# Attention sum of a sliding, dilated attention moved to (offset, head) on partitions, with the values re-laid through DRAM

## The chip, the cores and the metric

The kernel runs on one core of a Trainium2 chip. The metric is the device time of one execution in microseconds (us). The profiler's span of the same execution, first to last instruction, is 1 to 2 us shorter than that time, and positions inside the kernel are given on the span. A ratio is always the mean time of one kernel's fast runs over that of the other's fast runs of the same rounds on the same chip, so it is not quite the ratio of the medians that I quote.

TensorE does matrix multiplies, VectorE elementwise work, ScalarE evicts accumulators and does exponentials, GpSimd a few masks, and DMA queues move data. In the profile they are PE (with PEld for its weight loads), DVE, ACT, POOL and, for the queue that issues transfers, SP.

## The reference, cut to what matters

```python
# x: [2048, 640]; 32 heads of 20; window of 8 offsets with step 2
xn = layernorm(x)
q, k, v = split(xn @ wqkv)                     # each [32 heads, 2048, 20]
idx = pos[:, None] - 2 * arange(8)[None, :]    # position minus 0, 2, ... 14
logits = einsum("bhsd,bhswd->bhsw", q, k[idx]) * 20 ** -0.5     # masked where idx < 0
attn = softmax(logits, axis=-1)                # over the 8 offsets
o = einsum("bhsw,bhswd->bhsd", attn, v[idx])
h = (xn @ w_gate) * (xn @ w_up)                # gated part, inner size 1536
return x + o @ wo + h @ w_down
```

Softmax runs over 8 offsets only. The attention sum `o` is therefore no matrix product: it is, for each of 640 channels and 2048 positions, a sum of eight products.

## The kernel before

It keeps everything transposed: channel on partitions (five chunks of 128), position along the row. Attention weights are computed with (position block, head) on partitions, one row per offset `w`, in `LOG`. To multiply them with the values, they have to be repeated over the 20 channels of each head. That is done by TensorE with a 0/1 matrix `GTZ`, one matmul for each offset, chunk and block of 512 positions. Then ScalarE evicts, VectorE multiplies by the shifted values, and TensorE adds the eight products with an identity matrix:

```python
    units = [(w, c, j) for j in range(NJ) for c in range(NCH) for w in range(W)]     # 4 x 5 x 8 = 160

    def pv_E(u):
        ...
        op("pe", lambda e: e.matmul(PS[:, eb, :], GTZ[:, j, c, :], LOG[:, w, :], start=True, stop=True), ...)
        op("act", lambda e: e.activation(ES[:, es, :], PS[:, eb, :], ACT.Copy), ...)
        lo = PAD + j * JB - DIL * w
        op("dve", lambda e: e.tensor_tensor(PB[:, pb, :], ES[:, es, :], VTP[:, c, lo:lo + JB], ALU.mult), ...)

    def pv_I(u):
        ...
        op("pe", lambda e: e.matmul(PS[:, ob, :], IDENT[:], PB[:, pb, :], start=(w == 0), stop=(w == W - 1)), ...)
        if w == W - 1:
            op("act", lambda e: e.activation(QOT[:, c, j * JB:(j + 1) * JB], PS[:, ob, :], ACT.Copy), ...)
```

The order of work is: layer normalization together with the Q, K and V projections; the logit stage (40 VectorE products of 128x2048, each followed by four 32-column logit matmuls), with gate and up matmuls between; softmax; the attention stage above, with the rest of the gated part and the output projection between.

## Time and profile before

| | before |
|---|---|
| time, median of 4 runs | 352.55 us (351.58 to 353.38) |
| span of the profiled run | 351.9 us |
| TensorE busy | 334.8 us, 95% |
| VectorE, ScalarE busy | 60%, 58% |
| mean granted TensorE clock | 1.000 |

The profile's page of the kernel before: its busy line, the chain of work that ended last, and four of the costliest groups (line, engine, operation, output and inputs, count | busy us, mean ns of one | idle us just before them and who ended it).

```profile
PE 334.8 (95%) x1884; PEld 158.9 (45%) x1884; DVE 212.7 (60%) x438; ACT 203.2 (58%) x362; POOL 16.5 (5%) x43
...
PE 92%; DVE 5%; ACT 1%; DMA 1%; issue 0%; DVEq 0%; ACTq 0%
...
L592 ACT ACTIVATE ES<-PS 128x512 bf16<-128x512 f32 x160 | 88.3, 598 | 41.0 <-PE PS L590 41.0
L598 DVE TENSOR_TENSOR PB<-ES,VTP 128x512 bf16<-128x512 bf16 x160 | 67.4, 425 | 56.6 <-ACT ES L592 52.4
...
L590 PE MATMUL PS<-LOG,GTZ 128*128 128x512 bf16 x160 | 60.5, 379 | 0.5 <-ACT ES L592 0.5
L606 PE MATMUL PS<-PB,IDENT 128*128 128x512 bf16 x160 | 60.5, 379 | 0.0
```

The chain is 92% TensorE: nothing else matters until TensorE has less to do. In their attention groups ScalarE waits for TensorE (41 us idle) and VectorE for ScalarE's evictions (52 of its 57 us idle), while TensorE waits for ScalarE only 0.5 us. A mean of 379 ns does not mean that a matmul costs 379 ns, because matmuls overlap in the pipeline; the cost is read from the pace. The timeline of TensorE shows it (start us, us, engine, line, operation, count, and in brackets the idle time before):

```profile
16.70 6.21 PE L364 MATMUL PS<-XNT,RA 128*128 128x512 bf16 x15 [1.07 <-DVE XNT L355]
22.74 0.44 PE L349 MATMUL PS<-IDENT,XNS 128*128 128x128 bf16 x5
23.02 3.40 PE L364 MATMUL PS<-XNT,RA 128*128 128x512 bf16 x15
26.26 0.44 PE L349 MATMUL PS<-IDENT,XNS 128*128 128x128 bf16 x5
...
90.23 0.62 PE L389 MATMUL PS<-PRODW,G 128*32 128x512 bf16 x8
90.78 1.25 PE L500 MATMUL PS<-XNT,WG 128*128 128x512 bf16 x5
91.86 1.24 PE L526 MATMUL PS<-XNT,WU 128*128 128x512 bf16 x5
```

Differences of starts give the pace: five 512-column matmuls in 91.86 - 90.78 = 1.08 us, so 0.216 us each; eight 32-column logit matmuls in 0.55 us, so four run at a time. The first 15 projection matmuls take 22.74 - 16.70 = 6.04 us where the next 15 take 26.26 - 23.02 = 3.24: TensorE begins at about half pace.

### The profile page before, as it was taken

The page shows a single profiled execution, that of the slowest core. Times are in us where ns is not written, and L with a number is a line of the kernel's source. Part 1 is how long each engine was busy: PE and PEld are TensorE (multiplying, and loading weights), DVE is VectorE, ACT ScalarE, POOL GpSimd, SP SyncE. Part 2 cuts the span into 40 slices and gives each one's busy share as a digit, 9 for nine tenths or more (in the row PEclk, how much of TensorE's full clock was granted, in tenths as well). Part 3 has the DMA queues.
Part 4 walks back from the last instruction along what each step waited for, and adds up shares of the span by engine and source line. Part 5 has one row for each costly group of instructions (what it writes and reads, how often), then busy time and mean ns, then how long its engine had stood idle before and what let it go on. Part 6 is the DMA issues. An engine that isn't in the chain of part 4 may idle for free.

```text
span 351.9 us, 4822 instructions
## 1 busy us (share of the span) xinstructions
PE 334.8 (95%) x1884; PEld 158.9 (45%) x1884; DVE 212.7 (60%) x438; ACT 203.2 (58%) x362; POOL 16.5 (5%) x43
## 2 busy tenths in 40 slices
PE   1399999999999999999999999999999999999996
PEld 0245454444333333445444445544445444555553
DVE  5834541003899999647665657665585757556523
ACT  4557777555445454572477767667667676566400
POOL 8000000000200010000100000000000000000000
PEclk9999999999999999999999999999999999999999
DMA  7999100000200020001100001010001000000011
GB/s 213 340 395 365 46 2 0 0 2 0 75 2 0 2 75 2 0 0 39 38 0 2 0 0 39 20 58 19 19 20 37 20 2 0 21 19 19 20 37 39
DMA packets 11350, 17.47 MB, mean 50 GB/s; under 512 B 1296, under 2 KB 9488, under 8 KB 11328
## 3 DMA queue, kind: packets, MB, share of 16 engines
q1 hardware_dynamic: 10464, 14.42, 11.9%
q0 software_dynamic: 864, 2.75, 2.6%
q8 instruction: 15, 0.25, 0.3%
q14 instruction: 7, 0.06, 0.1%
HBM read 14.42 MB, written 2.62 MB: 48 GB/s over the span
## 4 chain that ended last, share of the span: by engine, by line
PE 92%; DVE 5%; ACT 1%; DMA 1%; issue 0%; DVEq 0%; ACTq 0%
PE PS L364 19%; PE PS L500 15%; PE PS L526 15%; PE PS L551 12%; PE PS L590 10%; PE PS L606 10%; PE PS L626 5%; PE PS L389 3%; PE PS L556 3%; PE PS L349 1%; DVE KTP L573 1%; DVE STATS L317 1%; DVE STATS L319 1%; DMA XST<-in_A_x_dram 1%; DVE XNT L355 0%; DVE NB L333 0%
## 5 line engine op out<-in xcount | busy, mean ns | idle before, releaser
L592 ACT ACTIVATE ES<-PS 128x512 bf16<-128x512 f32 x160 | 88.3, 598 | 41.0 <-PE PS L590 41.0
L598 DVE TENSOR_TENSOR PB<-ES,VTP 128x512 bf16<-128x512 bf16 x160 | 67.4, 425 | 56.6 <-ACT ES L592 52.4
L364 PE MATMUL PS<-XNT,RA 128*128 128x512 bf16 x300 | 69.5, 390 | 1.1 <-DVE XNT L355 1.1
L383 DVE TENSOR_TENSOR PRODW<-QOT,KTP 128x2048 bf16<-128x2048 bf16 x40 | 48.6, 1222 | 28.3 <-ACT KTP L377 19.6
L590 PE MATMUL PS<-LOG,GTZ 128*128 128x512 bf16 x160 | 60.5, 379 | 0.5 <-ACT ES L592 0.5
L606 PE MATMUL PS<-PB,IDENT 128*128 128x512 bf16 x160 | 60.5, 379 | 0.0
L500 PE MATMUL PS<-XNT,WG 128*128 128x512 bf16 x240 | 59.8, 380 | 0.0
L526 PE MATMUL PS<-XNT,WU 128*128 128x512 bf16 x240 | 59.6, 379 | 0.0
L551 PE MATMUL PS<-WD,RA 128*128 128x512 bf16 x192 | 46.0, 379 | 0.5 <-DVE KTP L573 0.5
L364 PEld LDWEIGHTS PS<-XNT,RA 128*128 128x128 bf16 x300 | 29.5, 100 | 36.0 <-issue 4.9
L526 PEld LDWEIGHTS PS<-XNT,WU 128*128 128x128 bf16 x240 | 23.5, 98 | 28.1
L500 PEld LDWEIGHTS PS<-XNT,WG 128*128 128x128 bf16 x240 | 21.7, 98 | 31.4 <-issue 8.5
L551 PEld LDWEIGHTS PS<-WD,RA 128*128 128x128 bf16 x192 | 18.6, 98 | 22.8 <-DVE KTP L573 1.1
L626 PE MATMUL PS<-WO,QOT 128*128 128x320 bf16 x160 | 27.0, 299 | 0.1
L504 ACT ACTIVATE KTP<-PS 128x512 bf16<-128x512 f32 x28 | 16.7, 597 | 12.7 <-PE PS L500 11.1
L606 PEld LDWEIGHTS PS<-PB,IDENT 128*128 128x128 bf16 x160 | 15.6, 98 | 16.8 <-DVE PB L598 1.7
L590 PEld LDWEIGHTS PS<-LOG,GTZ 128*128 128x128 bf16 x160 | 15.6, 98 | 16.1 <-ACT ES L592 1.2
L504 ACT ACTIVATE ES<-PS 128x512 bf16<-128x512 f32 x20 | 11.9, 597 | 18.2 <-PE PS L500 18.2
L626 PEld LDWEIGHTS PS<-WO,QOT 128*128 128x128 bf16 x160 | 15.5, 98 | 10.7 <-ACT QOT L609 0.5
L349 PE MATMUL PS<-IDENT,XNS 128*128 128x128 bf16 x80 | 8.4, 247 | 12.1 <-ACT XNS L341 12.1
L341 ACT ACTIVATE XNS<-XST,NB,RSTD 128x640 bf16<-128x640 bf16 x16 | 14.7, 920 | 7.4 <-DVE NB L333 7.4
L534 ACT ACTIVATE PB<-PS 128x512 bf16<-128x512 f32 x20 | 11.9, 597 | 9.6 <-PE PS L526 9.6
(61 smaller groups left out, 240.8 us busy)
## 6 DMA issues: line engine op xcount, KB each, us to landing
XST<-in_A_x_dram SPq DMA_DIRECT2D x16, 160.0 KB, 6.8
XST<-in_A_x_dram POOLq DMA_DIRECT2D x16, 160.0 KB, 2.5
out_dram<-FOUT SPq DMA_DIRECT2D x16, 160.0 KB, 1.8
RA<-in_A_wqkv_dram SPq DMA_DIRECT2D x3, 800.0 KB, 10.2
WG<-in_B_w_gate_dram SPq DMA_DIRECT2D x5, 384.0 KB, 10.7
WU<-in_B_w_up_dram SPq DMA_DIRECT2D x5, 384.0 KB, 11.1
WD<-in_B_w_down_dram SPq DMA_DIRECT2D x12, 160.0 KB, 8.8
WO<-in_A_wo_dram SPq DMA_DIRECT2D x5, 160.0 KB, 8.1
```

The source lines that it names most:

```text
L341: op("act", lambda e: e.activation(XNS[:, u, :], XST[:, slot, :], ACT.Identity, bias=NB[:, t:t + 1], scale=RSTD[:, t:t + 1]), reads=[("xst ...
L364: op("pe", (lambda c: lambda e: e.matmul(PS[:, kb, :], WQKV[:, c, m * 128:(m + 1) * 128], XNT[:, c, j * JB:(j + 1) * JB], start=(c == 0), ...
L383: op("dve", lambda e: e.tensor_tensor(PRODW[:, slot, :], QOT[:, c, :], KTP[:, c, lo:lo + S], ALU.mult), reads=rk, writes=[("prod", slot)], ...
L500: op("pe", (lambda c: lambda e: e.matmul(PS[:, gb, :], WG[:, c, m * 128:(m + 1) * 128], XNT[:, c, jg * JB:(jg + 1) * JB], start=(c == 0), ...
L504: op("act", lambda e: e.activation(gsx[:, gs, :], PS[:, gb, :], ACT.Copy), reads=psk(gb) + extra, writes=[gk], name=f"gev{m}_{jg}")
L526: op("pe", (lambda c: lambda e: e.matmul(PS[:, ub, :], WU[:, c, m * 128:(m + 1) * 128], XNT[:, c, jg * JB:(jg + 1) * JB], start=(c == 0), ...
L551: op("pe", (lambda m: lambda e: e.matmul(PS[:, bb, :], HT4[:, hb, m, rows], WD[:, m, 0:512], start=(m == 0), stop=(m == NF - 1)))(m), read ...
L590: op("pe", lambda e: e.matmul(PS[:, eb, :], GTZ[:, j, c, :], LOG[:, w, :], start=True, stop=True), reads=[("gtz", j)] + [("log", w, jq) fo ...
L592: op("act", lambda e: e.activation(ES[:, es, :], PS[:, eb, :], ACT.Copy), reads=psk(eb), writes=[("es", es)], name=f"Eev{w}_{c}_{j}")
L598: op("dve", lambda e: e.tensor_tensor(PB[:, pb, :], ES[:, es, :], VTP[:, c, lo:lo + JB], ALU.mult), reads=rk, writes=[("pb", pb)], name=f" ...
L606: op("pe", lambda e: e.matmul(PS[:, ob, :], IDENT[:], PB[:, pb, :], start=(w == 0), stop=(w == W - 1)), reads=[("ident",), ("pb", pb)], wr ...
L626: op("pe", (lambda c: lambda e: e.matmul(PS[:, ab, 0:DHALF], QOT[:, c, rows], WO[:, c, cols], start=(c == 0), stop=(c == NCH - 1)))(c), re ...
```

## The change

The intent is to take the 160 expansions and most of the 160 sums off TensorE. If (offset, head) lies on partitions, an attention weight is already beside all 20 channels of its head, and repeating it is a broadcast along the row, which VectorE can read directly. For that the values must be laid out with the offset on partitions too. V is stored four times into a DRAM scratch, each copy shifted by 2q positions (q = 0 to 3), and reloaded as `VX` with partition (q, head) and row (channel, position); offsets w = q and w = q + 4 are two views of the same row, 8 positions apart. Weights move on chip from `LOG` to `ATX`. VectorE makes products of 128 x (4 channels x 2 views x 512); TensorE sums over the four q with a 128 x 32 selection matrix, four channels side by side in column tiles.

```diff
-        op("pe", ... e.matmul(PS[:, eb, :], GTZ[:, j, c, :], LOG[:, w, :], start=True, stop=True) ...)   # x160
-        op("act", ... e.activation(ES[:, es, :], PS[:, eb, :], ACT.Copy) ...)                            # x160
-        op("dve", ... e.tensor_tensor(PB[:, pb, :], ES[:, es, :], VTP[:, c, lo:lo + JB], ALU.mult) ...)  # x160
-        op("pe", ... e.matmul(PS[:, ob, :], IDENT[:], PB[:, pb, :], ...) ...)                            # x160
+    def v_store(m):                                   # 20 stores of 512 KB
+        for q in range(4):
+            x0 = 8 + DIL * q
+            dma(vscr[q, m * 128:(m + 1) * 128, x0:x0 + S], VST[:, m, :], ...)
+    def vx_load(j):                                   # 4 reloads of 2600 KB
+        src = vscr.rearrange("q (h d) s -> (q h) d s", d=DH)[:, :, j * JB:j * JB + VW]
+        dma(VX[:, j % 2], src, ...)
+    def attn_move(j):                                 # 16 moves of 64 KB
+        for wq in range(4):
+            dma(ATX[32 * wq:32 * wq + 32, :, j * JB:(j + 1) * JB], LOG[32 * j: ...], ...)
+    def pv_mul(j, c):                                 # 20 products
+        vw = bass.AP(v.tensor, v.offset, [v.ap[0], [VW, 4], [8, 2], [1, JB]])
+        a = ATX[:, :, j * JB:(j + 1) * JB].unsqueeze(1).to_broadcast([128, 4, 2, JB])
+        op("dve", lambda e: e.tensor_tensor(P[:, u], vw, a, ALU.mult), ...)
+    def pv_sum(j, c):                                 # 20 units of 8 column-tiled matmuls
+        for r in range(2):
+            for dq in range(4):
+                o = PS[32 * dq:32 * dq + 32, b, :]
+                op("pe", ... e.matmul(o, SEL[:], P[:, u, dq, r, :], start=(r == 0), stop=(r == 1),
+                                      tile_position=(0, 32 * dq)) ...)
+        op("act", lambda e: e.activation(OT[:, c, ...], PS[:, b, :], ACT.Copy), ...)
```

Two more things change. The down projection and the output projection go into one accumulation of 17 matmuls of 320 columns. And the order of work is new: only Q and K are projected beside the layer normalization; V is projected in the logit stage. A list of filler work for TensorE (V, then gate and up, then down/output groups) is taken from as the attention advances:

```diff
+    for i, (w, c) in enumerate(order):                # logit stage
+        qk_prod(...); ...; qk_logits(...)
+        run_fill(1.05)
+    for st in softmax_steps():
+        st()
+        run_fill(1.05)
+    for j in range(2):
+        vx_load(j)
+    for j in range(NJ):
+        attn_move(j)
+    run_fill(12.0)
+    pv_mul(*units[0])
+    for i, (j, c) in enumerate(units):                # 20 units
+        run_fill(2.1)
+        if i + 1 < len(units):
+            pv_mul(*units[i + 1])
+        ...
+        pv_sum(j, c)
```

A down/output group of position block j may only start when the five units of that block are done.

## The prediction

> What bounds it now. TensorE: busy 334.8 of 351.9 us in the table of engines, 92% of the chain of waits, granted clock 1.00 throughout. From 16.7 us the timeline shows it back to back at a fixed pace: 0.216 us per 512-column matmul (five in 1.08), 0.136 per 320 columns, 0.056 per 128, and 0.27 for four 32-column-tiled logit matmuls (eight in 0.55). Start 16.7, about 2.8 extra on the first 15 matmuls (6.2 us; later groups take 3.4), work 325.6 and end 3.0 add to 348; the rest is small waits. VectorE (60%) and ScalarE (58%) have slack.
>
> What the change does on TensorE. Removed: 160 expansion matmuls (LOG,GTZ) and 160 identity sums (PB,IDENT), 320 x 0.216 = 69.1 us. Added: 160 column-tiled sums (SEL), 40 x 0.27 = 11.0 us if they overlap four deep as the logits do. Down (41.5+10.7) and output projection (21.7) become 544 matmuls of 320 columns, 73.9: unchanged. QKV, gate/up, logits: same counts. New work 267.5 us, 58 less. All of it was on the critical path.
>
> Other engines. ScalarE loses 160 evictions (88.3 us). VectorE loses 160 multiplies (67.4 us) and gains 20 of 128x4096: the existing attn multiply of that size with a broadcast took 2.28, so 46 us. It also loses copies of up (14.4). DMA gains 10.5 MB of scratch stores, 10.6 MB of reloads, 1 MB of attention moves; at the 360-390 GB/s seen in the load stage, 29 us of stores under the logit stage (66-120 us), 14 us of first reloads under softmax. The skill's page "DMA: Bandwidth & Descriptors", Specifications, gives about 358 GB/s of HBM per core[...]; no trace here has large stores.
>
> Where I expect new waits.
> 1. Normalization with 2 instead of 3 projection groups per tile: TensorE 2.44 us a tile, ScalarE's chain (0.62+0.83+2x0.48) about 2.45, VectorE 2.26. Nearly equal; 0-2 us lost.
> 2. Softmax (from ~120 us): chain of about 21 us including the 3.35 us reciprocal, h products between, then attention moves; first multiply near 145, first sum near 148. Fill work queued (26 groups, 28 us) just covers it. A later softmax or move stalls TensorE one for one.
> 3. Units 2-4: fill runs out (down of block 0 needs five units), so TensorE waits for VectorE's 2.3 us multiplies: about 5.5 us.
> 4. Units 5-19: TensorE 2.71-2.86 us a unit, VectorE 2.7-2.75: nearly balanced, 1-2 us lost.
> Sum: 16.7+2.8+267.5+3.0 = 290, plus 1+6.5+1 of waits and about 1.5 small losses: 299-300.
>
> Checks after: TensorE instructions 1884 to about 1724, work about 268 us; SEL groups of four in about 0.27; multiplies near 2.3; waits of TensorE on P in a window near 150-160 of about 5.5 us; no wait on the scratch reload; chain still mostly PE.
>
> What would make it wrong. Scratch stores (rows at offsets that are not 64-byte multiples) much slower than loads, or 1040-byte reload rows slow, so that units start late; the 16 attention moves taking more than about 4 us; multiplies over overlapping views at half the rate (4.5 us), which makes the unit stage VectorE-bound, about +30 us; TensorE gaps that drop its clock: the skill's "TensorE: Matmul & The Clock Gate", "Why this matters for your kernels", warns of idle gaps over about 3 us, the cold start of this trace shows the price (about 2.8 us each). Tiny padding stores could delay the weights. All push upward, hence the skewed range.
>
> Predicted 299 us, 8 in 10 between 291 and 311; faster by over 2%: 0.98, within 2%: 0.01, slower: 0.01.

## The result, and the profile after

The changed kernel took 299.48 us (median of 4 runs, 298.96 to 300.27) against 352.55 us before; the ratio of the fast runs is 0.8499, with a 95% interval of 0.8472 to 0.8527. The span of the profiled run is 298.2 us.

The page of the changed kernel, in the lines that answer to those shown of before:

```profile
PE 278.3 (93%) x1724; PEld 138.3 (46%) x1724; DVE 170.2 (57%) x266; ACT 129.0 (43%) x221; POOL 2.3 (1%) x17
...
PE 80%; DVE 11%; ACT 4%; DMA 2%; issue 1%; SPq 1%; DVEq 0%; ACTq 0%
...
L457 DVE TENSOR_TENSOR P<-VX,ATX 128x4096 bf16<-128x4096 bf16 x20 | 45.4, 2284 | 0.2 <-issue 0.2
...
L466 PE MATMUL PS<-P,SEL 128*32 128x512 bf16 x160 | 12.7, 396 | 4.2 <-DVE P L457 4.2
```

TensorE's two attention groups of 121 us busy have become one of 12.7, and the chain is now 11% VectorE: there is one place where TensorE waits for products, 4.2 us. The timeline of TensorE in the changed kernel, first at the start and then at that place:

```profile
15.97 3.68 PE L364 MATMUL PS<-XNT,WQKV 128*128 128x512 bf16 x10 [0.92 <-DVE XNT L351]
19.48 0.44 PE L345 MATMUL PS<-IDENT,XNS 128*128 128x128 bf16 x5
19.76 2.32 PE L364 MATMUL PS<-XNT,WQKV 128*128 128x512 bf16 x10
21.92 0.44 PE L345 MATMUL PS<-IDENT,XNS 128*128 128x128 bf16 x5
...
147.62 0.61 PE L466 MATMUL PS<-P,SEL 128*32 128x512 bf16 x8
...
150.43 0.62 PE L466 MATMUL PS<-P,SEL 128*32 128x512 bf16 x8
152.10 0.62 PE L466 MATMUL PS<-P,SEL 128*32 128x512 bf16 x8 [1.05 <-DVE P L457]
154.31 0.62 PE L466 MATMUL PS<-P,SEL 128*32 128x512 bf16 x8 [1.59 <-DVE P L457]
156.51 1.04 PE L466 MATMUL PS<-P,SEL 128*32 128x512 bf16 x8 [1.58 <-DVE P L457]
157.48 3.38 PE L513 MATMUL PS<-WD,HT 128*128 128x320 bf16 x12
...
162.13 0.61 PE L466 MATMUL PS<-P,SEL 128*32 128x512 bf16 x8
162.67 1.80 PE L513 MATMUL PS<-WD,HT 128*128 128x320 bf16 x12
...
165.09 0.61 PE L466 MATMUL PS<-P,SEL 128*32 128x512 bf16 x8
```

The eight sums of a unit take 0.55 us, as the logits do. Units 2, 3 and 4 (starts 152.10, 154.31, 156.51) follow each other at 2.2 us, the length of one VectorE product, because filler work has run out. And there is something the prediction did not expect: the first down/output group starts at 157.48 and ends at 162.13, 4.65 us, where the next takes 165.09 - 162.67 = 2.42. The granted clock says why. The windows view of the changed kernel (stretch, its length, busy us and instruction count of each engine, then the granted clock, DMA share and GB/s):

```profile
152.00:154.00 2.00, 0.62 (x8) 0.12 (x8) 2.00 (x2) 0.60 (x1) 0.00 (x0) 1.00 0.64 195
154.00:156.00 2.00, 0.62 (x8) 0.12 (x8) 2.00 (x2) 0.60 (x1) 0.00 (x0) 0.82 0.00 0
...
158.00:159.00 1.00, 1.00 (x5) 0.59 (x4) 0.99 (x2) 0.20 (x1) 0.00 (x0) 0.50 0.86 220
...
162.00:163.00 1.00, 1.00 (x12) 0.37 (x12) 0.77 (x2) 0.21 (x1) 0.00 (x0) 0.95 1.09 348
```

A mean of 0.82 over 154 to 156, made of 1.00 and 0.50, puts the drop at 155.28 us, about 0.3 us into the third wait; it ends at about 162.1. Between them TensorE ran at half its clock. That costs 4.65 - 2.42 = 2.2 us on the group and 0.97 - 0.55 = 0.4 us on the fifth sum, 2.65 us together. This is the cost in the profiled run, whose mean clock was 0.989. Of the other three runs one is like it (0.988) and two have 0.993 and are about 1 us shorter.

### The profile page after: what moved, and what is told of

Its sections match the earlier page's. It is cut to its first block, busy times and chain, and to the rows that moved or that the text cites. A ratio compares the mean times of both kernels' runs of the same rounds, so it can differ in the third digit from the quotient of the medians.

```text
span 298.2 us, 4200 instructions
## 1 busy us (share of the span) xinstructions
PE 278.3 (93%) x1724; PEld 138.3 (46%) x1724; DVE 170.2 (57%) x266; ACT 129.0 (43%) x221; POOL 2.3 (1%) x17
## 4 chain that ended last, share of the span: by engine, by line
PE 80%; DVE 11%; ACT 4%; DMA 2%; issue 1%; SPq 1%; DVEq 0%; ACTq 0%
PE PS L486 27%; PE PS L513 26%; PE PS L364 20%; PE PS L396 4%; DVE P L457 3%; PE PS L466 3%; DVE SM L409 1%; DMA v_scratch<-KT 1%; ACT LOG L423 1%; DVE RS L428 1%; PE PS L345 1%; DVE STATS L325 1%; ACT GSX L488 1%; DVE STATS L326 1%; DVE LOG L436 1%
## 5 line engine op out<-in xcount | busy, mean ns | idle before, releaser
L364 PE MATMUL PS<-XNT,WQKV 128*128 128x512 bf16 x300 | 69.5, 385 | 0.9 <-DVE XNT L351 0.9
L513 PE MATMUL PS<-WD,HT 128*128 128x320 bf16 x384 | 59.0, 305 | 0.0
L389 DVE TENSOR_TENSOR PRD<-QT,KT 128x2048 bf16<-128x2048 bf16 x40 | 47.0, 1220 | 18.9 <-ACT KT L369 14.7
L488 ACT ACTIVATE GSX<-PS 128x512 bf16<-128x512 f32 x48 | 28.8, 600 | 45.9 <-PE PS L486 32.3
L513 PEld LDWEIGHTS PS<-WD,HT 128*128 128x128 bf16 x384 | 37.5, 99 | 18.9 <-issue 3.8
L457 DVE TENSOR_TENSOR P<-VX,ATX 128x4096 bf16<-128x4096 bf16 x20 | 45.4, 2284 | 0.2 <-issue 0.2
L364 PEld LDWEIGHTS PS<-XNT,WQKV 128*128 128x128 bf16 x300 | 28.4, 99 | 36.3 <-issue 4.0
L493 DVE TENSOR_TENSOR HT<-USX,GSX 128x512 bf16<-128x512 bf16 x48 | 20.1, 423 | 38.8 <-ACT USX L488 38.7
L488 ACT ACTIVATE USX<-PS 128x512 bf16<-128x512 f32 x48 | 28.8, 601 | 20.5 <-PE PS L486 20.3
L513 PE MATMUL PS<-WO,OT 128*128 128x320 bf16 x160 | 27.7, 304 | 0.0
L466 PE MATMUL PS<-P,SEL 128*32 128x512 bf16 x160 | 12.7, 396 | 4.2 <-DVE P L457 4.2
```

Of the source, the lines that this page charges most:

```text
L364: op("pe", (lambda l, x, c: lambda e: e.matmul(PS[:, b, :], l, x, start=(c == 0), stop=(c == NCH - 1)))(l, x, c), r=[l, x], w=[PS[:, b, :] ...
L389: op("dve", lambda e: e.tensor_tensor(PRD[:, s, :], QT[:, c, :], k, ALU.mult), r=[QT[:, c, :], k], w=[PRD[:, s, :]], name=f"prod{w}_{c}")
L457: op("dve", lambda e: e.tensor_tensor(P[:, u], vw, a, ALU.mult), r=[v, ATX[:, :, j * JB:(j + 1) * JB]], w=[P[:, u]], name=f"pv{j}_{c}")
L466: op("pe", (lambda o, dq, r: lambda e: e.matmul(o, SEL[:], P[:, u, dq, r, :], start=(r == 0), stop=(r == 1), tile_position=(0, 32 * dq)))( ...
L488: op("act", lambda e: e.activation(X[:, k, :], PS[:, b, :], ACT.Copy), r=[PS[:, b, :]], w=[X[:, k, :]], name=f"guev{which}_{m}_{j}")
L493: h_pending.append(lambda: op("dve", lambda e: e.tensor_tensor(o, USX[:, k, :], GSX[:, k, :], ALU.mult), r=[USX[:, k, :], GSX[:, k, :]], w ...
```

## The experiments

Ratios to the changed kernel are quotients of the two ratios to the kernel before, because the changed kernel was not run again beside the experiments: e1 to e4, e5 to e8 and the last two ran on three chips. The third digit of such a quotient is uncertain by about 0.003 to 0.004. Ten kernels ran on the chip; all gave the reference's result except e6, which was wrong.

### e1: dummy matmuls in the three waits

```diff
+    def keep_warm(n):
+        b = bank()
+        for k in range(n):
+            op("pe", lambda e: e.matmul(PS[:, b, :], IDENT[:], XNT[:, 0, 0:JB], start=True, stop=True), ...)
...
+        if i in (2, 3, 4):
+            keep_warm(4 if i == 2 else 6)
         pv_sum(j, c)
```

> The changed kernel with 4, 6 and 6 dummy 512-column matmuls in the three TensorE waits of units 2 to 4 (nothing reads them). Theory: the first down group took 4.65 us instead of 2.42 because the granted clock fell to 0.5 after a stretch of TensorE only about a third busy; dummies hold the clock, so that group takes 2.4, the fifth sum 0.55 instead of 1.0, and the kernel gains 2.6 us: about 296.8, ratio to the changed kernel 0.991. The waits on P stay as long as before, dummies included. Rival: the slow group has another cause (its weights, its operands); then 4.65 stays and the time is 299 to 300 or a little more.

Measured: 297.70 us (5 runs), ratio to before 0.8445, to the changed kernel 0.9936; span 296.6. The timeline of TensorE in e1:

```profile
155.96 1.47 PE L623 MATMUL PS<-XNT,IDENT 128*128 128x512 bf16 x6
157.61 0.61 PE L466 MATMUL PS<-P,SEL 128*32 128x512 bf16 x8 [0.18 <-DVE P L457]
158.16 1.80 PE L513 MATMUL PS<-WD,HT 128*128 128x320 bf16 x12
...
160.57 0.62 PE L466 MATMUL PS<-P,SEL 128*32 128x512 bf16 x8
```

With the same operands and weights, the group now takes 160.57 - 158.16 = 2.41 us; the granted clock of the run is 1.000. From the first sum to the end of this group: 160.57 - 148.74 = 11.83 us, against 162.13 - 147.62 = 14.51 in the changed kernel. That is 2.68 us, the amount expected. Useless work made the kernel faster, so the cause is the clock, not the group's operands. The whole kernel gained less (1.8 us in the medians, 1.6 between the two profiled spans). In the profiled run the reason is that its first sum came 1.1 us later (148.74, not 147.62): the half-pace start took longer. The first ten projections took 4.24 us here and 3.51 in the profiled run of the changed kernel, from code that is the same. In the seven profiled runs without warm-up of the transposes, this start costs between about 1.4 us and 3 us more than full pace. The clock entries of the packed traces tell why: the clock came up at 18.73 us in the changed kernel's profile and at 22.07 in that of e1, and the extra time is half of what lies between the first projection and that moment (half of 2.76 and of 6.00 us). A difference of a microsecond between two single profiles is therefore not evidence; stretches inside the kernel are.

### e2: useful work in the three waits

The first 12 matmuls of a down/output group need no attention output. In e2 three groups get this part done in the waits, in banks that are held until the attention output is there.

```diff
+        if i in (2, 3, 4):
+            tail_head(*((0, 0), (0, 1), (1, 0))[i - 2])     # the 12 matmuls with WD of three groups
         pv_sum(j, c)
```

> The changed kernel with the first 12 matmuls (the down part, which needs no attention output) of three output groups done inside the three waits of units 2 to 4. Theory: waits of 4.2 us and the slow clock of 2.6 us go, about 6.5 to 7 us in all: 292.5, ratio to the changed kernel 0.977; the unit stage after it stays limited by TensorE or by VectorE at about 2.8 us a unit. Rival 1: the wait only moves to later units, because VectorE is the real limit of the unit stage: then gain under 3.5 us. Rival 2: the clock has another cause: gain about 4.

Measured: 295.64 us (5 runs), ratio to before 0.8396, to the changed kernel 0.988, a gain of 3.8 us. The three waits and the clock drop are gone, but a new wait has come up in unit 7. The timelines of e2 show it, first TensorE's, then VectorE's, then that of the issuing queue:

```profile
170.68 0.61 PE L466 MATMUL PS<-P,SEL 128*32 128x512 bf16 x8 [2.06 <-DVE P L457]
```

```profile
167.93 0.49 DVE L526 TENSOR_TENSOR FOUT<-PS,XR 128x320 bf16<-128x320 f32 x1 [2.51 <-issue]
168.34 2.28 DVE L457 TENSOR_TENSOR P<-VX,ATX 128x4096 bf16<-128x4096 bf16 x1
```

```profile
156.59 0.58 SPq L265 DMA_DIRECT2D VX<-v_scratch  x1
160.26 0.62 SPq L265 DMA_DIRECT2D out_dram<-FOUT  x1
```

TensorE waits for a product. On VectorE the product stands behind the output addition of tile 2, and VectorE sits idle for 2.5 us before that addition. The profile does not name what it waits for ("issue"). The group of tile 2 was finished at 165.6. There are two output buffers, so tile 2 reuses that of tile 0, whose store was issued at 160.26, 3.7 us after a 2.6 MB scratch reload that took 10.9 us to land. A store behind a reload on the same queue would land at about 167.5. The trace bears this out: the slowest of the 16 output stores took 7.6 us to land where the median is 1.8, and 160.26 + 7.6 is 167.9, when the addition starts. In the changed kernel the store of 177.6, also behind a reload, took 8.0 us, but nobody needed its buffer then. That the buffer is what VectorE waited for was still an inference; e9 tests it. So rival 1 was partly right: part of the gain was given back later, though not by VectorE's pace. The expected gain itself was there: from the first sum to the end of the span, e2 is 4.4 us shorter than the changed kernel (146.2 against 150.6), and with the 2.06 us of the new wait that makes 6.5.

### e3: the sums without column tiles

```diff
-                o = PS[32 * dq:32 * dq + 32, b, :]
-                ... e.matmul(o, SEL[:], P[:, u, dq, r, :], start=(r == 0), stop=(r == 1), tile_position=(0, 32 * dq)) ...
+                o = PS[:, b, :]
+                ... e.matmul(o, SELW[:, dq, :], P[:, u, dq, r, :], start=(dq + r == 0), stop=(dq + r == 4)) ...
```

`SELW[:, dq, :]` is 128 x 128, with the selection matrix in its columns 32 dq to 32 dq + 31 and zeros elsewhere.

> The changed kernel with each unit's eight 32-column matmuls, which run four at a time, replaced by eight 128-column ones into one accumulation (same result). Theory: the sums lie on TensorE's path; they cost 160 x 0.216 = 34.6 us instead of 40 x 0.275 = 11.0, +23.6; the waits of units 2 to 4 shrink by about 3.4 and the clock drop of 2.6 goes: net +17 to +18, about 317, ratio to the changed kernel 1.058. Rival: VectorE's 2.3 us multiply sets the pace of the units and hides the sums: +5 or less.

Measured: 316.41 us (4 runs), ratio to before 0.8973, to the changed kernel 1.056. TensorE in e3, unit 0 and the filler after it:

```profile
148.46 1.89 PE L471 MATMUL PS<-P,SELW 128*128 128x512 bf16 x8
150.18 1.24 PE L491 MATMUL PS<-XNT,WG 128*128 128x512 bf16 x5
```

The sums of a unit now take 1.72 us, and the waits of TensorE on products shrank to 1.0 us, without a drop of the clock. The sums lie on TensorE's path, and running four at a time is worth about 17 of the 53 us that the change won.

### e4: V projected in front of the logit stage

```diff
     for m in range(NCH):
         for j in range(NJ):
-            fill.append((1.08, lambda m=m, j=j: proj(2, m, j)))
-        fill.append((0.0, lambda m=m: v_store(m)))
+            proj(2, m, j)
+        v_store(m)
```

> The changed kernel with the value projections moved back in front of the logit stage, where the kernel before had them; the amount of work is the same. Theory: the chain from logits through softmax to unit 4 starts 21.6 us later and fill work ends that much too early, so TensorE waits about 21 us more between softmax and unit 4: about 321, ratio to the changed kernel 1.07. Rival: order hardly matters, since TensorE's sum of work is unchanged: within 3 us.

Measured: 319.95 us (4 runs), ratio to before 0.9071, to the changed kernel 1.067. TensorE in e4, the last filler group and unit 0:

```profile
149.51 1.24 PE L486 MATMUL PS<-XNT,WU 128*128 128x512 bf16 x5
168.33 1.04 PE L466 MATMUL PS<-P,SEL 128*32 128x512 bf16 x8 [17.57 <-DVE P L457]
```

The amount of work is the same, and TensorE now waits 22.2 us for products where it waited 4.2. In the long wait the clock falls too: it was 0.50 from 154.9 to 182.2 us. The order is not a detail: it is worth about 20 us here. It matters because the chain from the last logit through softmax to unit 4 is a VectorE and ScalarE chain of about 38 us (118.4 to 156.5 in the changed kernel), and every microsecond of filler used up before it is missing there.

### e5: softmax without the maximum

The logits of these inputs are small enough for exponentials without the maximum; the result agrees with the reference. For larger inputs this could overflow, so e5 tests the chain rather than offering an equivalent kernel.

```diff
-            tt(MX[:], LOG[:, 0:4, :], LOG[:, 4:8, :], ALU.max, "smax1"),
-            tt(MY[:], MX[:, 0:2, :], MX[:, 2:4, :], ALU.max, "smax2"),
-            tt(MZ[:], MY[:, 0, :], MY[:, 1, :], ALU.max, "smax3"),
...
-            steps.append(... e.tensor_tensor(L, L, bc(MZ[:], 4), ALU.subtract) ...)
```

> The changed kernel without the maximum and its subtraction in softmax (five VectorE instructions, 4.8 us; same mathematics, the result should agree). Theory: the chain from the last logits to the first multiply is VectorE's and ScalarE's, so units start about 4.5 us earlier (about 140 instead of 144.7), TensorE's waits in units 2 to 4 fall from 4.2 to about 1 us or less and the clock does not drop: 293 to 294.5, ratio to the changed kernel 0.981. Rival: attention moves or the scratch reload set the start of the units: then the first multiply stays near 144 and the time is unchanged.

Measured: 293.52 us (5 runs), ratio to before 0.8328, to the changed kernel 0.980. The first product starts at 138.91 instead of 144.68, there is no wait of TensorE on products among the listed waits, and the clock stays at 1.000. Neither the moves of the weights nor the reload held the start of the units: the softmax chain did.

### e6: the kernel before with short expansions

```diff
-        op("pe", lambda e: e.matmul(PS[:, eb, :], GTZ[:, j, c, :], LOG[:, w, :], start=True, stop=True),
+        op("pe", lambda e: e.matmul(PS[:, eb, 0:128], GTZ[:, j, c, :], LOG[:, w, 0:128], start=True, stop=True),
```

> The kernel before with its 160 expansion matmuls cut from 512 to 128 columns (result wrong on purpose; evictions and multiplies keep their sizes). Theory: only TensorE's columns bound that kernel, so it gains 160 x 0.16 = 25.6 us: about 327, ratio to the kernel before 0.928. Rival: the chain of eviction and multiply in the attention stage was as binding as TensorE: gain under 13 us.

Measured: 331.92 us (4 runs; wrong result), ratio to the kernel before 0.9419. Taking columns off TensorE alone gave 20.7 us, 80% of what was taken off. ScalarE's idle time before its 160 evictions fell, and TensorE's waits rose a little, in the group lines of e6:

```profile
L592 ACT ACTIVATE ES<-PS 128x512 bf16<-128x512 f32 x160 | 87.2, 601 | 25.1 <-PE PS L590 23.3
...
L606 PE MATMUL PS<-PB,IDENT 128*128 128x512 bf16 x160 | 55.5, 380 | 1.6 <-DVE PB L598 1.6
...
L590 PE MATMUL PS<-LOG,GTZ 128*128 128x128 bf16 x160 | 35.0, 220 | 0.8 <-ACT ES L592 0.8
```

So the kernel before was bound by TensorE's columns, but a change that had only shortened them would have begun to meet the eviction and multiply chain. The idle time of TensorE in the windows of the attention stage (3.0 us from 170 to 280 us, against 0.5 us in the kernel before from 160 to 320 us) accounts for about 2.5 us of the missing 5. The starts of the matmuls account for all of it: from the starts of the 160 expansions to those of the matmuls behind them it is 34.6 us in the kernel before and 13.9 in e6, 20.7 less, where 160 at the usual pace of 0.056 would take 9.0. The 4.9 us are thus waits behind the short expansions, about half of them hidden under the modelled ends of the matmuls.

### e7: every scratch store issued twice

```diff
             dma(dst, VST[:, m, :], r=[VST[:, m, :]], w=[("vscr", m, q)], name=f"vst{m}_{q}")
+            dma(vscr2[q, m * 128:(m + 1) * 128, x0:x0 + S], VST[:, m, :], ...)
```

> The changed kernel with every scratch store issued a second time to another scratch tensor (10.5 MB more). Theory: store and reload traffic is hidden; the reloads landed about 13 us before the first multiply, the added stores take about 28 us at 375 GB/s and move the reloads by 10 to 13 us: first multiply at 145 to 147, time 299 to 301. Rival: the DMA path has no such slack, or the traffic slows the engines: 305 or more.

Measured: 306.52 us (6 runs, 304.81 to 308.66), ratio to before 0.8696, to the changed kernel 1.023. My expectation fell and the rival's number came true. The timelines of VectorE and of the issuing queue in e7:

```profile
151.98 2.29 DVE L461 TENSOR_TENSOR P<-VX,ATX 128x4096 bf16<-128x4096 bf16 x1 [6.55 <-DMA ATX<-LOG]
```

```profile
130.14 4.15 SPq L267 DMA_DIRECT2D VX<-v_scratch  x2
140.55 12.44 SPq L267 DMA_DIRECT2D ATX<-LOG  x16
```

The reloads wait for the stores of the first scratch, which now share their queue with as many others. They were issued at 130.14 instead of 113.88, 16.3 us later, and the first product came at 151.98 instead of 144.68, 7.3 us later. So the DMA path of the changed kernel has 16.3 - 7.3 = 9 us of slack, not 13. The named releaser is the move of the weights, 64 KB each: in the same queue they stand behind 5.3 MB of reload, so they pay for its lateness. TensorE's wait for the first product then brings clock drops of its own (0.50 from 152.8 to 159.6 and from 163.0 to 169.8 us). The traffic is hidden in the changed kernel, but only by 9 us.

### e8, e9, e10b: better versions

e8 is e2 with two more edits. The padding of the scratch had been stored from the first columns of the K tile, and this held up the first K eviction; e8 stores it from a zero tile. And it puts dummy matmuls among the first transposes.

```diff
-            z = KT[:, :, 0:x0]
+            z = ZP[:, :, 0:x0]
...
+        warm(9)                    # nine 128-column matmuls on the identity
         ln_pe(t)
+        if t == 4:
+            warm(8)
```

> Candidate for the best version: e2, plus padding stores from a zero tile of their own (they held back the first K eviction by 1.9 us and TensorE by 0.41), plus dummy matmuls among the first transposes so that the clock is up when the projections start (first ten took 3.51 us instead of 2.16). Theory: 0.4 and 1.35 us less than e2: about 290.8, ratio to the changed kernel 0.971. If the dummies do not count as activity at this density, only 0.4 less than e2.

Measured: 293.87 us (4 runs), ratio to before 0.8336, to the changed kernel 0.981, so 1.8 us less than e2. The expectation of 290.8 was reckoned from the 292.5 expected of e2, and it is too low by the 3.1 us by which e2 itself missed; the wait that e2 had kept, 2.2 us in unit 7 here, is most of that. ScalarE's line in the changed kernel, and TensorE's start in e8:

```profile
22.27 0.60 ACT L369 ACTIVATE KT<-PS 128x512 bf16<-128x512 f32 x1 [1.92 <-DMA v_scratch<-KT]
```

```profile
15.96 2.33 PE L366 MATMUL PS<-XNT,WQKV 128*128 128x512 bf16 x10 [0.72 <-DVE XNT L353]
18.12 0.44 PE L347 MATMUL PS<-IDENT,XNS 128*128 128x128 bf16 x5
```

The first ten projections take 2.16 us, full pace, and no ScalarE instruction waits for the padding store any more.

e9 is e8 with a third output buffer. A version with four, and the same combination without the maximum, did not build because they did not fit into the on-chip memory; both went in again with three.

```diff
-    FOUT = sb("FOUT", [128, 2, D])
+    FOUT = sb("FOUT", [128, 3, D])
```

> e8 with three output buffers instead of two, nothing else (four did not fit into the on-chip memory and failed to build). Theory: what e2 and e8 gave back is one wait of 2.1 to 2.2 us in unit 7: VectorE could not write the output of tile 2, because the store of tile 0 (same buffer) sat in the DMA queue behind the 2.6 MB scratch reload; with three buffers tile 2 has its own, the wait goes and the kernel takes about 291.7, ratio to e8 0.993. Rival: VectorE's pace in the unit stage, not the store, made the wait; then it stays or moves to a neighbouring unit and the time is 293 to 294.

Measured: 292.31 us (5 runs, 291.45 to 292.77), ratio to before 0.8284 (0.8265 to 0.8303), to e8 0.994. TensorE in e9, at its start and at the place where e2 and e8 waited:

```profile
15.95 3.26 PE L366 MATMUL PS<-XNT,WQKV 128*128 128x512 bf16 x10
19.05 0.44 PE L347 MATMUL PS<-IDENT,XNS 128*128 128x128 bf16 x5
...
166.64 0.84 PE L522 MATMUL PS<-WO,OT 128*128 128x320 bf16 x5
167.41 0.61 PE L468 MATMUL PS<-P,SEL 128*32 128x512 bf16 x8
```

The wait is gone and did not move to another unit: no wait of TensorE on products is listed, although one output store still took 7.4 us to land. This confirms the store behind the reload. The first two lines show a loss of 0.94 us in the profiled run, which is 0.6 us above the expectation: the clock had come up during the transposes (11.04 us), fell again before the projections (14.45 to 17.87), and the first ten took 3.10 us. Whether the other runs, with about the same median, lost it there too is not shown. In e8's profiled run the same dummies had sufficed; the section on the prediction says what told the two apart.

e10b is e5 with the zero tile, the warm start and three output buffers.

> e5 (no maximum in softmax) with the padding zero tile, the warm start and three output buffers; no early down matmuls. Theory: the cold start (about 2 us in e5's profile) and the 0.4 us of the held-back K eviction go: about 291.2, the span near 289.3, TensorE then without a wait on P of more than 0.3 us.

Measured: 292.02 us (4 runs, 291.26 to 292.22), ratio to before 0.8275 (0.8258 to 0.8292). This is 0.8 us above the expectation. No wait of TensorE on products is listed; its first ten projections took 3.25 us, 1.09 more than at full pace, again with a clock that had fallen (14.72 to 18.13). e9 and e10b cannot be told apart by their intervals. Both beat both kernels, by about 2.5% over the changed one; e9 keeps the softmax as it was.

## Why the prediction was right

The prediction said 299 us, and 299.48 were measured. The total agrees better than its terms do; some errors cancelled, which is luck. Its sum of 299 to 300 is also one of positions on the span, so it is to be compared with 298.2; that it met the time of 299.48 owes 1.7 us to the difference between span and time, which the sum does not contain. The terms, in us of the profiled span:

| term | predicted | measured | how |
|---|---|---|---|
| start of the projections | 16.7 | 15.97 | timeline |
| half-pace start | 2.8 | 1.35 | 3.51 - 2.16 for the first ten |
| wait in the normalization stage | about 1 | 0.41 | waits of TensorE |
| waits of units 2 to 4 | 5.5 (6.5 in its sum) | 4.2 | waits of TensorE |
| clock drop after them | 0, named as a risk | 2.65 | 2.2 + 0.4, undone in e1 |
| TensorE work, unit-stage and small losses | 267.5 + 1 + 1.5 | 270.8 | the rest of the span |
| end | 3.0 | 2.8 | last matmul at 295.4 |

- **Bound by TensorE's columns, before.** Right. e6 gave back 80% of the columns that it took off the kernel before, and column tiling alone is worth 17 us (e3).
- **58 us of TensorE work less.** Right: busy time fell by 56.5 us, from 334.8 to 278.3, with 1724 instructions as said, sums in groups of four at 0.27 us.
- **Products at 2.3 us.** Right: 2284 ns. Overlapping views with a broadcast operand ran at the rate of the existing 128x4096 multiply with a broadcast.
- **DMA hidden.** Right in the result. The stores ran at 366 GB/s on average in the stretch from 70 to 98 us, and no product waited for the reload. e7 shows a slack of 9 us. The figure of about 358 GB/s that the prediction took from the skill's page is no ceiling here, with one core running: the loads of the kernel before moved 393 to 404 GB/s from 16 to 24 us.
- **Softmax just covered, then a wait in units 2 to 4.** Right in place and cause: first product at 144.68 (said 145), first sum at 147.62 (said 148), 4.2 us of waits (said 5.5). The order that covers it is worth about 20 us (e4), and shortening the softmax chain removes the wait (e5).
- **The clock.** This is the step that failed in detail. The prediction priced a clock drop as a risk of idle gaps over about 3 us and added nothing for gaps of less than 2. The gaps were 1.05 and 1.59 us, and the clock fell early in the third. What counted was not one long gap: in the 3.41 us before 155.28 (the length of the activity window that the page "TensorE: Matmul & The Clock Gate" of the Trainium skill gives in Part 1) TensorE was busy for 1.23 us, 36%, while in the stretch of the same length before 151.05 it was busy throughout. The mis-sized term is the drop's 2.65 us; it was offset by a cheaper start (1.45 and 0.7 us less) and a shorter wait (1.3 us less). The cheaper half-pace start is luck: it depends on the moment at which the clock came up (e1).
- **The clock, in all twelve traces.** The clock entries of the packed traces let the windows be placed: between two changes of the clock there is always a whole number of 3.413 us (two from 155.27 to 162.09). Measured on its own run's windows, the clock fell after windows in which TensorE was busy for 36% (the changed kernel), 39% (e9), 42% (e7) or 44% (e10b) or less, and it stayed up after 50% or more (50% in e2 and e8, 52% and 56% in e8). Single gaps of 2.06 and 2.24 us in e2 and e8 left it at 1.00. It came up after 81% or more and not after 76% (e1). So e8, e9 and e10b differ with the same dummies because their windows lay differently, and where they lie changed from run to run of the same code. The shares rest on modelled ends of matmuls, and no run was made to find the limits.
- **Normalization stage.** The size (0.41 us) was inside the range, but the cause was another: the balance of engines held, and the wait came from the padding stores, which the prediction had suspected of delaying weights and which delayed an eviction.
- **Unit stage.** Said 2.71 to 2.86 us of TensorE a unit plus losses of 1 to 2 us in all; measured 2.81 and 2.96. A down/output group takes 2.42 us beside column-tiled sums and 34.64 / 15 = 2.31 from start to start in the run of 16 at the end, so about 0.1 us is lost before each unit's sums, 2 us over 20 units; in e3, where the sums are not column-tiled, the same group takes 2.31 (160.56 to 162.87). A second 0.1 us is inside the sums' 0.55: twelve logit matmuls in the changed kernel take 0.77 (110.70 to 111.47), so four more cost 0.22 and not 0.27. The prediction's price had that part in it.

Where the page "TensorE: Matmul & The Clock Gate" of the Trainium skill speaks of the start, in Part 1, it calls the activity window free-running and the number of slow matmuls run-variable. The runs here agree: the half-pace start costs 1.35 to about 3 us for the same code.

## What to carry to other kernels

When TensorE is the bound, look for matmuls that only repeat or add data; a layout in which the repetition is a broadcast read and the sum fits into column tiles can take them off, if the re-layout's DMA has an earlier stage to hide in. Then the new limit is where filler work runs out, so keep filler for the serial chain (here softmax), and keep TensorE densely busy there: three waits of 1.6 us or less cost 2.65 us more in the profiled run, through the clock, than their own length, and whether such waits do so depends on how busy TensorE is in a window that the kernel cannot place. When a wait is removed, look again downstream; here it let a small store fall behind a large reload in the queue, and a third buffer was needed to keep the gain.

## What the Trainium skill lacked or had wrong

- "TensorE: Matmul & The Clock Gate", section "Why this matters for your kernels", advises "No PE-idle gaps >~3µs between matmul bursts". Here gaps of 1.05 and 1.59 us and the start of a third, with sums of 0.62 us between, halved the clock for almost 7 us, and single gaps of 2.06 (e2) and 2.24 us (e8) did not. Filling the gaps kept the clock at 1.000 (e1). The busy share of a window tells these cases apart: the clock fell at 44% or less and stayed at 50% or more. Part 1 of the page has the window, and a case in which frequent short idle times make the clock swing, but no share.
- The same page, Part 1, gives a warm-up of about 3.4 us of sustained activity. It does not say that a window of partial work, after the clock has come up, can lower it again: with dummies among the transposes the first ten projections took 2.16 us in one profiled run (windows 50% and 56% busy) and 3.10 and 3.25 in two others (39% and 44%).
- "TensorEngine Tiling (Array Packing)", section "Key Properties", says that a change of tiling mode drains TensorE, without a figure. Here a change to column tiles and back came to about 0.1 us each (2.42 against 2.31 us for a group of 17; 0.55 us for eight sums where four more cost 0.22). That it is the drain is not shown.
- "DMA: Bandwidth & Descriptors", section "Queues, rings and completion order", says that descriptors are consumed in ring order on each engine, which agrees with what was seen. It gives no example of the cost: a 160 KB store, 1.8 us as a rule, took 7.6 us to land behind a 2.6 MB reload (e2), and a third buffer removed the wait (e9).
- "TensorE: Matmul & The Clock Gate", Part 1, warns that the recorded clock events are not fully to be trusted. It does not say that they can be missing at the start: the granted clock reads 1.00 for the stretch from 16 to 18 us of the changed kernel, while the matmuls there go at half pace (ten in 3.51 us instead of 2.16, over a stretch that the full clock joins at its end), and the trace's first clock entry begins only at 18.73 us. The pace of a known matmul is the safer reading there.
- No page that I read has a rate for large stores whose rows start off a 64-byte multiple: the stretch of the scratch stores (rows of 4096 bytes, shifted by 4 bytes from copy to copy) moved 366 GB/s.
